# A fused linear-attention and squared-ReLU FFN kernel: the last token tile's FFN-out in two column halves, copied by two engines and stored from two queues

## The chip, the cores and the metric

The kernel runs on one core of one Trainium2 chip. A core has five engines, each with its own in-order instruction queue: TensorE (PE: matmuls, and PEld: the loading of a matmul's stationary operand), VectorE (DVE), ScalarE (ACT), GpSimd (POOL) and SyncE (SP), which only issues DMAs and handles semaphores. Matmul results land in PSUM, which has eight banks of 128 rows x 512 f32; the other engines copy from there to SBUF, and DMAs move data between SBUF and HBM. The metric is device time in microseconds (us).

## The reference

There are 8 batches, 8 heads, a sequence of 576 and a head dimension of 64. A learned feature map turns q and k into 256 features, linear attention follows, and its output (4608 tokens of 512) goes through an FFN with a squared ReLU.

```python
def phi(x):
    proj = np.einsum('bhsd,df->bhsf', x, w_phi)               # d = 64, f = 128
    proj = proj - np.max(np.abs(proj), axis=-1, keepdims=True)
    return np.concatenate([np.exp(proj), np.exp(-proj)], axis=-1)
q_p, k_p = (phi(q), phi(k))
kv = np.einsum('bhsf,bhsd->bhfd', k_p, v)
z = np.sum(k_p, axis=2)
num = np.einsum('bhsf,bhfd->bhsd', q_p, kv)
den = np.einsum('bhsf,bhf->bhs', q_p, z)[..., None] + 1e-06
x = (num / den)              # -> [4608, 512]
h = np.maximum(x @ w_in, 0.0)        # w_in [512, 2048]
return (h * h @ w_out).astype(np.float32)   # w_out [2048, 512]
```

## The kernel before

Attention is worked batch by batch (eight batches). Its feature matmuls contract over the 64 of the head dimension, so they use 64 rows of TensorE (lines 496, 588, 634 and 666); the numerator matmuls (L734), the transposes (L438, L765) and the whole FFN use 128 rows. The FFN works on token tiles of 128, in nine chunks of four tiles. FFN-in (L796) makes, for a chunk, 16 PSUM banks of 128 hidden units x 512 tokens, four matmuls each; ScalarE applies the ReLU (L801), and GpSimd, in the last chunks VectorE, squares it (L804, L807). FFN-out (L825) makes, for one token tile, one bank of 128 tokens x 512 outputs from 16 matmuls. These are given to the planner as four parts of four matmuls. VectorE copies the bank to an `ot` buffer (L832, a ring of two), and SyncE stores it as two DMAs of 64 rows (L837), since the two halves of a tile belong to different places in the output.

The order of instructions on each engine is written by a small planner, the class `Plan` (line 46). Every piece of work is an `op` with an engine, a planned cost, a latency until others may use its result, a sorting key, dependencies and the buffers that it takes. `order` plays the plan forward: each free engine takes the ready op with the lowest key for which buffers are free. The instructions are then written out in the order of their planned starts, and the waits between engines follow from which data and buffers they share, in that order. Planned times thus set only the order; the chip's own times come out of the waits.

For TensorE, `pick` (line 80) chooses between ops of 64 and of 128 rows, since a change between the two costs time. With `now` as the lowest key of the ready 128-row ops, it changes to 64 rows when the first of them is overdue (`LATE`), or when the first lies under `now + EARLY[0]` and the ready ones up to `now + EARLY[1]` sum to `GROUP`, 400 ns of work; it stays there as long as keys lie under `now + AHEAD`. While TensorE has nothing to do before the first FFN input is there, `fill` (line 51) puts warm-up matmuls (L392) into the plan, every 240 ns from 500 to 5500 planned ns.

Latencies depend on `slack`: 40 ns and 200 ns in the first two attention batches (`M0`), and `MARGIN` for the later ones and for the FFN. TensorE's latency is 350 ns where slack is 100 or more.

At the start GpSimd issues the loads of batch 0's k, v and q in pieces, then the weights (`FIRSTS`, line 368), and builds an identity matrix. SyncE loads w_phi (L342), VectorE fills constants (L329 to L332) and converts w_phi (L344), and ScalarE loads its function table (L337).

Of the kernel before, what the change touches and what calls it, by code (L numbers as in the profile page):

```python
# [45 lines left out]
class Plan:  # L46
# [2 lines left out]
        self.idle = {}  # L49

    def fill(self, eng, cost, period, fn, until):
        self.idle[eng] = [cost, period, fn, until, 0.0]

    def op(self, eng, cost, key, fn, deps=(), bufs=(), lat=0, rows=None):

# [19 lines left out]
    SWITCH = 96  # L75

    AHEAD, GROUP, LATE = 24, 400, 8
    EARLY = 3, 8

    def pick(self, q, rows, can):  # L80
        now = min((it[0] for it in q if it[2].rows == 128), default=None)
# [5 lines left out]
        else:  # L87
            go = half[0][0] < now - self.LATE
            if not go and half[0][0] < now + self.EARLY[0]:
                free, work = {}, 0  # L90
                for it in half:
                    if it[0] > now + self.EARLY[1]:
                        break
# [106 lines left out]
def kernel(  # L200
# [10 lines left out]
    nc = tc.nc  # L211

    B, H, S, D = q.shape
    Fd = w_phi.shape[1]
    DM, DF = moe_w_in.shape
    P = 128
    NPR = H // 2
    NJ = S // 64
    U = NPR * NJ
    M = U // 2  # L220
    KC1, KC2 = DM // P, DF // P
# [8 lines left out]
    def ring(name, n, shape, dtype, pool=sb):  # L230
        return Ring([pool.tile(shape, dtype, name=f"{name}{i}") for i in range(n)])

    wphi2 = sb.tile([P, Fd], BF16, name="wphi2")
    win = sb.tile([P, KC1, DF], BF16, name="win")
    wout = sb.tile([P, KC2, DM], BF16, name="wout")
    ident = sb.tile([P, P], BF16, name="ident")
    wphi_f = sb.tile([P, Fd], F32, name="wphi_f")
# [10 lines left out]
    r_ksh = ring("ksh", 2, [P, 2, 4, Fd], F32)  # L248
# [12 lines left out]
    r_ot = ring("ot", 2, [P, DM], F32)  # L261
# [10 lines left out]
    r_out = Ring([0, 1])  # L272

    pl = Plan()
    MARGIN = 200
    M0 = 40, 200, 350
    slack = [M0[0]]
    att = []
# [1 line left out]
    def pe(key, cost, fn, deps=(), bufs=(), rows=128):  # L280
        o = pl.op("pe", cost, key, fn, deps, bufs, lat=350 if slack[0] >= 100 else 240, rows=rows)
        att.append(o)
        return o

    def act(key, n, fn, deps=(), bufs=()):
        return pl.op("act", 60 + 0.83 * n, key, fn, deps, bufs, lat=220 - 70 * (slack[0] < 100) + slack[0])

    def dve(key, n, fn, deps=(), bufs=()):

        return pl.op("dve", 65 + 1.04 * n, key, fn, deps, bufs, lat=190 - 60 * (slack[0] < 100) + slack[0])  # L290
# [13 lines left out]
    def load(key, kb, rows, fn, deps=(), bufs=()):  # L304

        n = (queue[-1][0] if queue else 0) + rows
        full = [d for m, d in queue if m >= n - 4096][:1]
        i = pl.op("pool", 780, key, fn, list(deps) + (full if n > 4096 else []), bufs, lat=0)  # L310
        issues.append(i)
        d = pl.op("dma", kb * 3, key, None, [i], bufs, lat=2600)
        queue.append((n, d))
        return d
# [5 lines left out]
    def store(key, fn, deps=(), bufs=()):  # L320
        return pl.op("sp", 1200, key, fn, deps, bufs, lat=2400)

    pl.op("pool", 1250, -1e9, None)


    FIRST = -1000

    def begin():
# [5 lines left out]
                    "x (h m p) -> x h m p", h=2, p=64)[:, :, M], 0.0)  # L334

    o_begin = dve(FIRST - 2, 400, begin)
    act(FIRST - 2, 1400, lambda: nc.scalar.activation(  # L337
        out=scrap[:, 4:8], in_=scrap[:, 0:4], func=ACT.Exp), [o_begin])

    def ld_wphi():  # L340
        for e in range(2):
            nc.sync.dma_start(out=wphi_f[e * 64 : e * 64 + 64, :], in_=w_phi)  # L342

    o_wphi = dve(FIRST - 1, 130, lambda: nc.vector.tensor_copy(out=wphi2, in_=wphi_f),  # L344
                 [store(FIRST, ld_wphi)])

    src = {"k": (k, r_xk), "v": (v, r_xv), "q": (q, r_xq)}
    got = {}

    def load_x(b, name, key, dep=None, a=0, z=NPR):  # L350

        t, r = src[name]
        if (b, name) not in got:
            got[b, name] = Buf(r), []
        buf, parts = got[b, name]
        rows = t[b].rearrange("h s d -> (h s d)").rearrange("(pr t c) -> t pr c", pr=NPR, t=P)

        def fn():
            nc.gpsimd.dma_start(  # L359
                out=buf.t[:, a * NJ : z * NJ].rearrange("t (pr j) d -> t pr (j d)", j=NJ),  # L360
                in_=rows[:, a:z, :],
            )
        parts.append((a * NJ, load(key, 295 * (z - a), 128 * (z - a), fn, [dep], [buf])))

    win_v = moe_w_in.rearrange("(kc p) m -> p kc m", p=P)
# [5 lines left out]
    for n, what in enumerate(FIRSTS.split()):  # L371
        what, a = what.split(":")
        a, z = (int(x) for x in a.split("-"))
        at = FIRST + n if n < NEXT else -160 + n
        if what == "win":
            x = slice(a * P, z * P)
            o = load(at, 262 * (z - a), 512, lambda x=x: nc.gpsimd.dma_start(
                out=win[:, :, x], in_=win_v[:, :, x]))
            o_win.update({mc: o for mc in range(a, z)})
        elif what == "wout":  # L380
            o = load(at, 262 * (z - a), 128 * (z - a),
                     lambda a=a, z=z: nc.gpsimd.dma_start(out=wout[:, a:z], in_=wout_v[:, a:z]))
            o_wout.update({mc: o for mc in range(a, z)})
        else:
            load_x(int(what[1]), what[0], at, None, a, z)

    def loads(b, dep):
        for name in "kvq":
            load_x(b, name, 32 * b - 120, dep)
# [10 lines left out]
    chunks = [4] * 9  # L400
    first = [sum(chunks[:c]) for c in range(len(chunks))]
# [4 lines left out]
    jord = [pairs + [NJ - 1], [NJ - 1] + pairs]  # L406
# [8 lines left out]
    def attention(b, key):  # L415
# [43 lines left out]

        slack[0] = M0[b] if b < 2 else MARGIN  # L460
        tk = transposes(xk, lk, kT, 0)
# [7 lines left out]

        slack[0] = M0[b] if b < 2 else MARGIN  # L470
        nf = FG[b] if b < len(FG) else 0
# [311 lines left out]
    h2 = {}  # L783
# [29 lines left out]
    outv = out.rearrange("(b p j) n -> b j p n", p=64, j=NJ)  # L813
    op_buf, stores = {}, []

    def ffn_out(c, i, key):
        tt, part = i // 4, i % 4
        if part == 0:
            op_buf[0] = Buf(r_one), Buf(r_out)
        w, out_ = op_buf[0]  # L820
        mcs = range(part * 4, part * 4 + 4)

        def fn():
            for mc in mcs:
                nc.tensor.matmul(  # L825
                    out=w.t, lhsT=h2[c, mc, tt][0].t[:, h2[c, mc, tt][1] :][:, :P], rhs=wout[:, mc, :],
                    start=(mc == 0), stop=(mc == KC2 - 1))
        p_ = pe(key, 865, fn, [h2[c, mc, tt][2] for mc in mcs] + [o_wout[mc] for mc in mcs],
                [w, out_] + [h2[c, mc, tt][0] for mc in mcs])
        if part == 3:  # L830
            o = Buf(r_ot)
            d = dve(key - 2, 560, lambda: nc.vector.tensor_copy(out=o.t, in_=w.t), [p_], [w, out_, o])  # L832

            def fn():
                for u in range(2):
                    g = 2 * (first[c] + tt) + u
                    nc.sync.dma_start(out=outv[g // NJ, jord[g // NJ % 2][g % NJ]],  # L837
                                      in_=o.t[u * 64 : u * 64 + 64, :])
            stores.append(store(key, fn, [d], [o]))
# [4 lines left out]
    n = 0  # L844
# [40 lines left out]
    att.clear()  # L885
    slack[0] = MARGIN
    for n, (what, c, i) in units:
        (ffn_out if what else ffn_in)(c, *i, n)

    for o in paced:  # L890
        n = int(o.key) - LEAD
# [37 lines left out]
```

## Time and profile before

| what | value |
|---|---|
| four runs, median (lowest to highest) | 359.88 us (359.48 to 360.7) |
| the profiled execution, its own time | 359.71 us |
| its span in the profile | 357.9 us |
| TensorE busy | 347.6 us, 97% |
| VectorE, ScalarE, GpSimd busy | 246.2, 240.5, 187.0 us |
| granted TensorE clock | 1.0 |
| end of the last matmul | 353.28 us |
| end of the last VectorE copy | 354.00 us |

Times in the profile are microseconds from the start of the span. A group's row gives line, engine and operation, what is written and read with shape (partitions x elements) and type, the count, the busy time and the mean of one. Matmuls are pipelined: the mean of one (0.38 us for 512 columns) is the time from start to end, while the next starts 0.216 us after it. A timeline row gives start, duration, the instruction, and in brackets the idle time of the engine before it and what ended it. The chain of waits follows the work that ended last back to the start, and names the piece of work that each stretch of time went to.

### The profile page before, as it was taken

What the parts mean: (1) busy time and instruction counts of PE and PEld (TensorE: products, weight loads), DVE (VectorE), ACT (ScalarE), POOL (GpSimd) and SP (SyncE); (2) the same over time, 40 slices, a digit from 0 to 9 for tenths busy, and PEclk for the clock granted to TensorE, in tenths of its full rate; (3) what the DMA queues carried; (4) which work ended last, traced back from release to release, by engine and by line L of the source; (5) the groups of instructions that cost most, each with busy time, mean ns of one, the idle gap of its engine ahead of it and who ended that gap; (6) DMA issues with size and microseconds to landing.
All of it is one profiled execution on the core that took longest, in us unless ns stands there. A gap on an engine that the chain in (4) does not pass through costs nothing.

```text
span 357.9 us, 10261 instructions
## 1 busy us (share of the span) xinstructions
PE 347.6 (97%) x4051; PEld 198.3 (55%) x4051; DVE 246.2 (69%) x556; ACT 240.5 (67%) x485; POOL 187.0 (52%) x293
## 2 busy tenths in 40 slices
PE   8799899999999999999999999999999999999994
PEld 6669676676754555455545554555455544444441
DVE  2988978796889489867687789777977843333321
ACT  2898988589829972997569776896588833333300
POOL 8836964557827981689547754786536400000000
PEclk9999999999999999999999999999999999999999
DMA  7999982557945875479648756695441331121133
GB/s 101 203 210 208 208 154 60 90 83 129 204 91 107 143 138 105 94 125 205 105 88 146 160 114 88 115 196 104 83 97 33 68 69 29 29 59 31 29 76 71
DMA packets 68816, 39.79 MB, mean 111 GB/s; under 512 B 48672, under 2 KB 63136, under 8 KB 68768
## 3 DMA queue, kind: packets, MB, share of 16 engines
q0 software_dynamic: 15872, 18.35, 31.3%
q1 hardware_dynamic: 52896, 20.79, 29.5%
q8 instruction: 31, 0.51, 0.6%
q14 instruction: 17, 0.14, 0.1%
HBM read 36.77 MB, written 9.44 MB: 129 GB/s over the span
## 4 chain that ended last, share of the span: by engine, by line
PE 90%; DVE 4%; DMA 2%; ACT 2%; issue 1%; POOL 0%; POOLq 0%; DVEq 0%
PE one L796 35%; PE one L825 35%; PE one L734 6%; PE one L588 5%; PE one L496 3%; PE one L666 3%; PE one L634 3%; DMA xk<-in_k_dram 2%; DVE mk L507 1%; ACT qph L641 1%; PE one L438 1%; DVE m L673 1%; DVE qT L446 0%; DVE ksh L517 0%; POOL xk L359 0%
## 5 line engine op out<-in xcount | busy, mean ns | idle before, releaser
L804 POOL TENSOR_TENSOR h<-hr 128x512 bf16<-128x512 bf16 x112 | 115.3, 1041 | 81.2 <-ACT hr L801 75.6
L796 PE MATMUL one<-xT,win 128*128 128x512 bf16 (+2 forms) x768 | 145.1, 326 | 0.2 <-DVE m L687 0.2
L825 PE MATMUL one<-wout,h 128*128 128x512 bf16 x576 | 144.7, 379 | 0.4 <-DVE xo L755 0.3
L801 ACT ACTIVATE hr<-one 128x512 bf16<-128x512 f32 x144 | 85.0, 608 | 77.7 <-PE one L796 72.5
L796 PEld LDWEIGHTS <-win 128*128 128x128 bf16 x768 | 65.9, 98 | 49.3 <-issue 1.1
L825 PEld LDWEIGHTS <-h 128*128 128x128 bf16 x576 | 52.6, 98 | 58.5 <-issue 1.7
L641 ACT ACTIVATE qph<-one 128x512 bf16<-128x512 f32 (+1 forms) x160 | 77.0, 577 | 6.1 <-PE one L634 6.0
L525 ACT ACTIVATE kph<-ksh 128x1024 bf16<-128x1024 f32 (+1 forms) x68 | 61.2, 956 | 6.0 <-DVE ksh L517 5.8
L507 DVE TENSOR_REDUCE mk<-one 128x4 f32<-128x512 f32 (+1 forms) x80 | 49.6, 628 | 6.3 <-PE one L496 6.1
L687 DVE TENSOR_REDUCE m<-one 128x4 f32<-128x512 f32 (+1 forms) x60 | 35.3, 632 | 18.7 <-PE one L666 11.6
L517 DVE TENSOR_TENSOR ksh<-one,mk 128x512 f32<-128x512 f32 (+1 forms) x68 | 42.8, 629 | 3.6
L832 DVE COPY ot<-one 128x512 f32<-128x512 f32 x36 | 24.7, 687 | 29.3 <-PE one L825 29.3
L734 PEld LDWEIGHTS <-qph 128*128 128x128 bf16 x640 | 29.1, 97 | 15.9 <-issue 3.1
L734 PE MATMUL one<-kv_sb,qph 128*128 128x65 bf16 x640 | 33.6, 194 | 1.7 <-DVE one L744 1.4
L744 DVE TENSOR_TENSOR one<-one,em 128x260 f32<-128x260 f32 (+1 forms) x80 | 31.9, 429 | 4.3 <-PE one L734 3.8
L755 DVE TENSOR_TENSOR xo<-one,rden 128x256 bf16<-128x256 f32 (+1 forms) x80 | 31.6, 418 | 0.7
L807 DVE TENSOR_TENSOR h<-hr 128x512 bf16<-128x512 bf16 x32 | 13.6, 424 | 21.9 <-ACT hr L801 21.9
L696 POOL COPY mq<-m 64x4 f32<-64x4 f32 x108 | 20.2, 187 | 13.0 <-DVE m L687 9.6
L588 PE MATMUL one<-va,kph 64*128 64x65 bf16 x1152 | 23.6, 190 | 0.8 <-POOL va L555 0.8
L588 PEld LDWEIGHTS <-kph 64*128 64x128 bf16 x1152 | 21.1, 94 | 3.2 <-issue 3.0
L751 DVE RECIPROCAL rden<-one 128x4 f32<-128x4 f32 (+1 forms) x80 | 12.6, 175 | 14.2 <-PE one L734 13.8
L666 PE MATMUL one<-wphi,qT 64*128 64x128 bf16 x296 | 15.5, 217 | 0.3 <-DVE ksh L517 0.2
(45 smaller groups left out, 202.0 us busy)
## 6 DMA issues: line engine op xcount, KB each, us to landing
out_dram<-ot SPq DMA_DIRECT2D x72, 128.0 KB, 2.4
xk<-in_k_dram POOLq DMA_DIRECT2D x7, 576.0 KB, 6.6
xv<-in_v_dram POOLq DMA_DIRECT2D x7, 576.0 KB, 9.3
xq<-in_q_dram POOLq DMA_DIRECT2D x7, 576.0 KB, 12.2
win<-in_moe_w_in_dram POOLq DMA_DIRECT2D x2, 1024.0 KB, 15.7
wout<-in_moe_w_out_dram POOLq DMA_DIRECT2D x2, 1024.0 KB, 24.9
xv<-in_v_dram POOLq DMA_DIRECT2D x2, 288.0 KB, 7.3
xq<-in_q_dram POOLq DMA_DIRECT2D x2, 288.0 KB, 8.8
```

The lines of the kernel that those rows point to most:

```text
L507: nc.vector.tensor_reduce(out=mk.t[:, e, ms], in_=wv(e), axis=AX.X, op=ALU.max, apply_absolute_value=True)
L517: nc.vector.tensor_tensor(out=ksh.t[:, e, : n // 2, :], in0=wv(e), in1=mk.t[:, e, ms].to_broadcast([P, n // 2, Fd]), op=ALU.subtract)
L525: nc.scalar.activation(out=t.t[:, :, : n // 2, :].rearrange("x e i f -> x e (i f)"), in_=ksh.t[:, :, : n // 2, :].rearrange("x e i f -> x ...
L588: nc.tensor.matmul(out=kvp(w, hi)[:, 2 * prl + s], lhsT=kph[g][s].t[r, i % 2, i // 2, :], rhs=va[s if g < nf else 0].t[r, u, : D + 1], sta ...
L641: nc.scalar.activation(out=t.t.rearrange("f (r b) hi p -> f b r hi p", b=2)[:, bk, :, :, lo:hi_], in_=w[bk].t[:, : nj * 256].rearrange("f ...
L687: d1 = [dve(kk, nj * 256, lambda w=w, m0=m0, nj=nj, bk=bk: nc.vector.tensor_reduce(out=m0.t[:, bk, : 2 * nj], in_=w[bk].t[:, : nj * 256].r ...
L734: nc.tensor.matmul(out=w.t[:, z * P : z * P + D + 1], lhsT=qg[s].t[:, h // 2, h % 2, :], rhs=kv[r][0].t[:, z % 2, z // 2, s, :], start=(s ...
L744: nc.vector.tensor_tensor(out=x, in0=x, in1=em.t[lo:hi_, hs].to_broadcast(list(x.shape)), op=ALU.mult)
L796: nc.tensor.matmul(out=w.t[:, y * n : (y + 1) * n], lhsT=win[:, kc, mc * P : (mc + 1) * P], rhs=xT.t[:, a:z, kc, :], start=(kc == 0), stop ...
L801: o = act(key - 4, TCH, lambda: nc.scalar.activation(out=r.t, in_=w.t, func=ACT.Relu), [p_], [w, r])
L804: o = pool(key - 4, 1050, lambda: nc.gpsimd.tensor_tensor(out=t.t, in0=r.t, in1=r.t, op=ALU.mult), [o], [r, t])
L825: nc.tensor.matmul(out=w.t, lhsT=h2[c, mc, tt][0].t[:, h2[c, mc, tt][1] :][:, :P], rhs=wout[:, mc, :], start=(mc == 0), stop=(mc == KC2 - 1))
```

## The change

The last token tile's FFN-out keeps its four parts, but the first two parts now make columns 0 to 255 (eight of the 16 matmuls each, 256 columns wide) and the last two make columns 256 to 511, all in the same PSUM tile. After each half, VectorE copies rows 0 to 63 and ScalarE rows 64 to 127 of that half to an `ot` buffer; SyncE stores the former and ScalarE's own queue stores the latter. Other tiles are as they were.

With it come changes to the planner's numbers and to the start. Warm-up matmuls begin at 1100 planned ns. `EARLY` is (3.3, 7) for (3, 8), and `MARGIN` 220 for 200. The planner assumes that ScalarE and SyncE can't start before 740 ns and VectorE not before 500, as it did with 1250 for GpSimd. The op of the ScalarE table and the chain of w_phi are given to the planner after the loads, and the w_phi load has a planned latency of 1600 for 2400. `load_x` gets a branch that would load pieces over SyncE or ScalarE, for the pieces that `EARLY_X` lists; `EARLY_X` is empty.

```diff
     def fill(self, eng, cost, period, fn, until):
-        self.idle[eng] = [cost, period, fn, until, 0.0]
+        self.idle[eng] = [cost, period, fn, until, 1100.0]
...
-    EARLY = 3, 8
+    EARLY = 3.3, 7
...
-    MARGIN = 200
+    MARGIN = 220
...
-    pl.op("pool", 1250, -1e9, None)
+    for e, c in (("pool", 1250), ("act", 740), ("sp", 740), ("dve", 500)):
+        pl.op(e, c, -1e9, None)
...
-    act(FIRST - 2, 1400, lambda: nc.scalar.activation(
+    o_table = lambda: act(FIRST - 2, 1400, lambda: nc.scalar.activation(
...
-    o_wphi = dve(FIRST - 1, 130, lambda: nc.vector.tensor_copy(out=wphi2, in_=wphi_f),
-                 [store(FIRST, ld_wphi)])
+    o_wphi = lambda: dve(FIRST - 1, 130, lambda: nc.vector.tensor_copy(out=wphi2, in_=wphi_f),
+                         [pl.op("sp", 1200, FIRST, ld_wphi, lat=1600)])
...
+    EARLY_X = {}
...
+        if (b, name, a) in EARLY_X:
...
+            return
...
+    o_table()
+    o_wphi = o_wphi()
...
-        mcs = range(part * 4, part * 4 + 4)
+        end = c == len(chunks) - 1 and tt == chunks[c] - 1
+        mcs = range(part % 2 * 8, part % 2 * 8 + 8) if end else range(part * 4, part * 4 + 4)
+        cols = slice(part // 2 * 256, part // 2 * 256 + 256) if end else slice(0, DM)
 
         def fn():
             for mc in mcs:
                 nc.tensor.matmul(
-                    out=w.t, lhsT=h2[c, mc, tt][0].t[:, h2[c, mc, tt][1] :][:, :P], rhs=wout[:, mc, :],
-                    start=(mc == 0), stop=(mc == KC2 - 1))
+                    out=w.t[:, cols], lhsT=h2[c, mc, tt][0].t[:, h2[c, mc, tt][1] :][:, :P],
+                    rhs=wout[:, mc, cols], start=(mc == 0), stop=(mc == KC2 - 1))
...
-        if part == 3:
+        if end and part % 2:
+            o = Buf(r_ot)
+            for u, copy, eng in ((0, nc.vector.tensor_copy, nc.sync), (1, nc.scalar.copy, nc.scalar)):
+                rows = slice(u * 64, u * 64 + 64)
+                d = (act if u else dve)(key - 2, 256, lambda copy=copy, rows=rows: copy(
+                    out=o.t[rows, cols], in_=w.t[rows, cols]), [p_], [w, out_, o])
+                g = 2 * (first[c] + tt) + u
+
+                def fn(eng=eng, rows=rows, g=g):
+                    eng.dma_start(out=outv[g // NJ, jord[g // NJ % 2][g % NJ]][:, cols],
+                                  in_=o.t[rows, cols])
+                stores.append(pl.op("act" if u else "sp", 620, key, fn, [d], [o], lat=2400))
+        elif part == 3:
```

More of the change, by code (lines that the diff above doesn't have):

```diff
@@ L362, in fn @@
             )
+        if (b, name, a) in EARLY_X:
+            eng, n = EARLY_X[b, name, a]
+            stage = Buf(r_ksh)
+            flat_x = lambda: stage.t.rearrange("x e i f -> x (e i f)")[:, : (z - a) * NJ * D]
+            def fn():
+                (nc.scalar if eng == "act" else nc.sync).dma_start(
+                    out=flat_x().rearrange("t (pr c) -> t pr c", c=NJ * D), in_=rows[:, a:z, :])
+            i = pl.op(eng, 640, FIRST - 3 + n, fn, [], [stage, buf], lat=0)
+            d = pl.op("dma", 295 * (z - a) * 3, FIRST - 3 + n, None, [i], [stage, buf], lat=1400)
+            for e, (lo, hi) in enumerate(((0, 5), (5, NJ))):
+                def fn(e=e, lo=lo, hi=hi):
+                    (nc.scalar.copy if e else nc.vector.tensor_copy)(
+                        out=buf.t[:, a * NJ + lo : a * NJ + hi].rearrange("t j d -> t (j d)"),
+                        in_=flat_x()[:, lo * D : hi * D])
+                parts.append((a * NJ, (act if e else dve)(
+                    FIRST + 2 + n, (hi - lo) * D, fn, [d], [stage, buf])))
+            return
         parts.append((a * NJ, load(key, 295 * (z - a), 128 * (z - a), fn, [dep], [buf])))
```

## The prediction

> **What bounds the kernel now.** I read the page first, then busy time by stretches, then the chain of waits, and last the end and the start instruction by instruction.
>
> The page, its first lines and the slices of TensorE:
>
> ```profile
> span 357.9 us, 10261 instructions
> PE 347.6 (97%) x4051; PEld 198.3 (55%) x4051; DVE 246.2 (69%) x556; ACT 240.5 (67%) x485; POOL 187.0 (52%) x293
> ...
> PE   8799899999999999999999999999999999999994
> ```
>
> TensorE is the bound everywhere but in the first tenth and in the last slice. Busy time by stretches (us and number of instructions for each engine) says it more sharply:
>
> ```profile
> 40.00:60.00 20.00, 18.64 (x337) 13.12 (x337) 16.22 (x38) 18.32 (x44) 13.17 (x14) 1.00 0.74 129
> ...
> 140.00:180.00 40.00, 40.00 (x468) 21.03 (x464) 29.08 (x67) 29.91 (x59) 27.54 (x44) 1.00 0.75 127
> 180.00:220.00 40.00, 40.00 (x474) 21.04 (x469) 33.34 (x71) 30.18 (x57) 24.92 (x41) 1.00 0.66 121
> ...
> 338.60:353.30 14.70, 14.67 (x68) 6.46 (x66) 3.10 (x5) 0.60 (x1) 0.00 (x0) 1.00 0.33 72
> 353.30:357.90 4.60, 0.00 (x0) 0.00 (x0) 0.69 (x1) 0.00 (x0) 0.00 (x0) 1.00 0.26 57
> ```
>
> From 60 us to 353.3 us TensorE has no idle time to give back; the last 4.6 us hold one VectorE copy and stores. So a change can win in three places only: the last 4.6 us, the start, and, in between, in how TensorE's own work is put together. What that means is seen in the chain of waits (start, duration, what) of an ordinary stretch:
>
> ```profile
> 183.80 0.55 PE one L496 x16
> 184.35 0.97 PE one L796 x4
> 185.32 0.86 PE one L825 x4
> 186.18 0.86 PE one L796 x4
> ```
>
> Four FFN matmuls of 512 columns take 0.86 us (0.216 each); the four that follow a stretch of 64-row attention matmuls (L496, L588, L634, L666) take 0.97. A change of row height thus costs 0.11. Matmul by matmul I count 17, 18, 17 and 20 such changes in the four 40 us from 100 to 260 us, and 98 from 60 to 280 us.
>
> The end, chain and then timeline (SPq is SyncE's DMA issuing):
>
> ```profile
> 339.89 13.39 PE one L825 x62
> 353.28 0.03 issue
> 353.31 0.69 DVE ot L832
> ```
>
> ```profile
> 349.85 0.69 DVE L832 COPY ot<-one 128x512 f32<-128x512 f32 x1 [2.76 <-PE one L825]
> 350.57 4.56 SPq L837 DMA_DIRECT2D out_dram<-ot  x4
> 353.31 0.69 DVE L832 COPY ot<-one 128x512 f32<-128x512 f32 x1 [2.76 <-PE one L825]
> ```
>
> **The last tile before.** Let S be the start of its first matmul. 16 matmuls at 0.216: the last starts at S+3.24 and ends 0.38 later (mean of one, 379 ns), S+3.62. Copy: 0.03 to start, 0.69 long: S+4.34. SyncE issues the two 64-row stores one behind the other, 354.02 and 354.54: the second at S+4.89. From issue to landing the trace gives 2.25 and 2.36 for the two: S+7.25. From that landing to the end of the span 1.04: S+8.29, so S is at 349.65.
>
> **Part 1, the last tile after.** 32 matmuls of 256 columns in place of 16 of 512, in order: first half 16, second half 16. Their price is that of FFN-in's 256-column form: eight in 0.87 (0.109 each, own weight load hidden), one alone 273 ns. Without waits the 32 would take as long as the 16. But both halves lie in one PSUM tile. The planner sets the copies of the first half 350 ns (its latency for TensorE) after part 1 ends, while part 2 (planned at 865 ns) starts at once; so the written order is part 0, 1, 2, then the two copies, then part 3. If engines that touch the same PSUM bank are kept apart, the copies wait for part 2 and part 3 waits for the copies. The trace has nothing where TensorE writes one half of a bank while the other half is read, so I bound it: no wait at one end, the whole round trip at the other. The nearest rows are the numerator matmuls L734, which stood 0.80 until VectorE's L744 on their bank was done and started 0.04 after it, and L825, which stood 0.30 for VectorE's L755. They are other uses of the same kind of tile, but all wait; I take the wait.
>
> With it: 24 matmuls, the last starts at S+23 x 0.109 = S+2.51, ends S+2.78. Copies of 64 rows x 256 columns start at S+2.81. VectorE: 64x256 from PSUM took 0.419 in L755, 128x256 0.417 in L687, so 0.42, to S+3.23. ScalarE: 128x256 took 0.390 in L641, to S+3.20. I take the two to run side by side, since they read different rows; the other end is one behind the other. TensorE restarts at S+3.27: part 3's last matmul starts at +0.76, ends S+4.31. Behind the waiting matmul are only these eight. Copies to S+4.76 (VectorE) and S+4.73. Stores 0.03 later, now one each on SyncE and ScalarE, S+4.79; landing at 2.25 S+7.04; closing 1.04, S+8.08. **That is 0.21 less than S+8.29.** The parts: copy -0.27, second issue and its slower landing -0.63, TensorE's stall +0.65 (3.27 where the next start was due at 2.62), the matmuls' last end and rounding +0.04.
>
> Here a rule of the Trainium skill speaks against the change: "PSUM — Partial Sum Buffer", section on bank collisions, says that two engines must not touch one bank within the same 32 partitions at once, whatever the columns, and that different 32-partition groups may. By it the stall is certain and the two copies by rows may overlap, so the sum would be -0.21; by the other end of my bounds it would be -0.75.
>
> No wait at all: last matmul ends S+3.65. The second half takes the `ot` buffer of the tile before, whose stores landed at 352.83 and 353.45 (S+3.80), so the ScalarE copy can't start before S+3.83, ends S+4.22, is stored at S+4.25 and lands S+6.50: S+7.54, or -0.75. With the wait this buffer is free in time and costs nothing. One copy behind the other (ScalarE waits for VectorE, 0.43 more, twice): part 3 ends at S+4.74, last copy at S+5.62, landing 7.90 to 8.01, S+8.94 to 9.05: +0.7.
>
> The DMAs: SyncE issued 2 stores for the tile and issues 2 still; two go past it to ScalarE's queue. SyncE's first-half store goes at S+3.26, is issued in 0.59 at most, and its queue is free at S+4.79. ScalarE has no other work after 340 us (0.60 in the whole stretch above), so its copies and issues have cover. No DMA issued by ScalarE is in the trace: bounds are SyncE's own, 2.0 at least and 3.5 at most (the two small w_phi loads), so -0.2 to +1.1 around the stores' 2.25; I take the stores', the same rows to the same place.
>
> **Part 2, the start.** The warm-up matmuls of TensorE begin in the plan at 1100 ns, not 0. Planned arrival of the first piece of k is 1250+780+885+2600 = 5515; before, one at 0, one at 500 and then every 240 make 22, and the trace has 22. After it: 1100+240n < 5515, 19.
>
> ```profile
> 1.20 4.87 PE L392 MATMUL one<-ones 128*128 128x256 bf16 x22 [1.20 <-DVE scrap L330]
> ...
> 5.86 0.63 PE L438 MATMUL one<-ident,xk 128*128 128x128 bf16 x4
> ...
> 9.30 0.34 PE L438 MATMUL one<-ident,xk 128*128 128x128 bf16 x3 [0.55 <-DMA xk<-in_k_dram]
> ```
>
> At this point one takes 0.213, so three fewer free 0.64; the first k had landed at 4.69. But TensorE then stands idle for the third k load (landed 9.25, the piece of 6.18 us in the chain), and all later work follows from 9.30. The cover of the 0.64 is that load, whose issue on POOL is not moved. So 0; bounds -0.64 (all carried through) and +0.3 (a warm-up matmul or two put in front of an attention one). Moving the ScalarE table load and the w_phi conversion in the list, and the three start costs (740, 740, 500), changes planned times only: each is the first ready work of its engine either way. `EARLY_X` is empty, so its branch, with its loads and copies, issues nothing: 0.
>
> **Part 3, the order of the middle.** `MARGIN` 220 for 200 puts 20 ns on every planned ACT, DVE and POOL latency of FFN and of batches 2 to 7. TensorE's waits on others from 60 to 338 us sum to 0.2, so there is nothing for it to win; it hides under FFN matmuls at hand. `EARLY` 3.3, 7 for 3, 8 changes when TensorE may leave the FFN for a 64-row stretch: sooner (3.3 units ahead), but counting less work as ready (up to 7). One pulls to shorter stretches, the other to longer. The price is 0.11 a change, their number unknown. Bounds: all 40 us like the best (17) or the worst (20) or three beyond, +-3 changes x 5.5 x 0.11 = +-1.8. I take 0, in the middle, as the two limits pull apart. In the second batch (30 to 62 us) TensorE's waits for VectorE sum to 1.7; a new order may move those by some tenths either way.
>
> **Sum.** -0.21 + 0 + 0: span 357.7 for 357.94. The profiled execution took 359.71, 1.8 outside the span and 0.17 under the median 359.88. Forecast of the median: 359.7. What a measurement of this kernel tells from no change is about 0.3%, 1.08 us.
>
> **The rivals.**
> - *More changes of row height.* `EARLY`'s first number opens 64-row stretches before enough attention work is at hand, and they come out shorter. For it: 20 changes in 220 to 260 us where neighbours have 17. Against: the wait for 400 ns of ready work stays. Decides from 12 more changes (+1.3 - 0.2); at 2.5 per 40 us, 14 more: +1.5 - 0.2, **361.2**. This is the case on the slower side.
> - *Fewer changes*, through the second number: 12 fewer, -1.3 - 0.2, **358.4**.
> - *The start is carried through.* For it: k landed 1.2 before its transposes. Against: the idle time for the third load. -0.64 - 0.21, **359.0**.
> - *The copies go one behind the other*: +0.7, **360.6**. For it: both read one bank; against: different rows.
> - *The halves overlap*: the wait is my own reading and the change does all that two halves suggest; TensorE runs on while the first half is copied, -0.75, **359.1**. For it: the halves share no column. Against: every wait of L734 and L825 on a bank in use.
>
> **How the numbers follow.** Forecast 0.33, more changes 0.22, fewer 0.17, copies in turn 0.12, start 0.09, no wait 0.07. Faster by over 0.3%: nearly all of fewer (0.16), half of start (0.05, with a little help of the order), 0.03 from the rest: 0.24. Slower: more changes 0.20, part of copies in turn (0.06, with some more changes), 0.01: 0.27. Within: 0.49. Forecast and the two cases of the tail hold 359.1 to 360.6; eight in ten need both order cases: 358.2 (fewer changes, some of the start) to 361.5 (more changes, some of the copies in turn).
>
> **What would show it.** After: an idle time of TensorE of 0.6 to 0.7 in the last 4 us, ended by VectorE or ScalarE, and none of it if the no-wait case holds. VectorE copies of 0.42 and ScalarE copies of 0.39, starting together. Last landing 2.2 to 2.4 after both issues. Nineteen matmuls in the first warm-up row, and still an idle TensorE ended by the k load at about 9.3. The end of TensorE's work against 353.28: +0.7 from the stall, and all beyond it is the start and the changes of row height, which can be counted. The prediction is wrong if that count moves by more than ten, or if a store issued by ScalarE takes well over 2.4 to land.

## The result

| | before | after |
|---|---|---|
| timed runs, median (lowest to highest) | 359.70 us (358.67 to 360.97) | 360.67 us (359.56 to 362.55) |
| ratio to before, 95% interval | | 1.0028 (1.0019 to 1.0037) |
| span of the profiled execution | 357.94 us | 358.36 us |
| start of the first `ot` copy of FFN-out | 57.86 us | 57.30 us |
| start of the last tile's first matmul | 349.65 us | 349.92 us |
| from there to the end of the span | 8.29 us | 8.44 us |

The changed kernel is slower by 0.28%, about 1.0 us (0.7 to 1.3), where the prediction had it 0.2 us faster. That is small, but the interval leaves out 1: the loss is real. The last line of the table shows that the part the change is named for gives nothing; the two lines above it show that more is lost between 57 and 350 us (292.61 in place of 291.79), after a gain at the start.

The page of the kernel after, its first lines, TensorE's slices and the row of FFN-out:

```profile
span 358.4 us, 10307 instructions
PE 347.6 (97%) x4064; PEld 199.8 (56%) x4064; DVE 247.6 (69%) x557; ACT 243.5 (68%) x487; POOL 186.4 (52%) x293
...
PE   8799899999999999999999999999999999999994
...
L851 PE MATMUL one<-wout,h 128*128 128x512 bf16 (+1 forms) x592 | 144.6, 374 | 1.3 <-DVE ot L860 0.9
```

At this height nothing has moved, but for the new idle time at the end of the last row: 0.9 us in which FFN-out waits for the `ot` copies. (Line numbers move with the edits: FFN-out is L825 before and L851 here.) The end of the same kernel in the timeline (start, duration, instruction, in brackets the idle time before it and what ended it):

```profile
352.74 0.37 ACT L860 COPY ot<-one 64x256 f32<-64x256 f32 x1 [13.25 <-PE one L851]
353.13 0.55 ACTq L865 DMA_DIRECT2D out_dram<-ot  x1
353.14 0.42 DVE L860 COPY ot<-one 64x256 f32<-64x256 f32 x1 [2.33 <-ACT ot L860]
353.58 2.41 SPq L865 DMA_DIRECT2D out_dram<-ot  x2
353.61 1.03 PE L851 MATMUL one<-wout,h 128*128 128x256 bf16 x8 [0.91 <-DVE ot L860]
...
354.68 0.37 ACT L860 COPY ot<-one 64x256 f32<-64x256 f32 x1 [1.57 <-PE one L851]
355.07 0.48 ACTq L865 DMA_DIRECT2D out_dram<-ot  x1
355.08 0.42 DVE L860 COPY ot<-one 64x256 f32<-64x256 f32 x1 [1.52 <-ACT ot L860]
```

ScalarE copies its rows, and only then VectorE, whose wait is ended by `ACT ot`. TensorE's last eight matmuls start after both: 353.607, where the matmul before them had started at 352.429 and the next was due 0.109 later, so they are 1.07 late. The second pair of copies goes in turn again.

The start:

```profile
1.20 4.24 PE L416 MATMUL one<-ones 128*128 128x256 bf16 x19 [1.20 <-DVE scrap L331]
5.23 0.63 PE L462 MATMUL one<-ident,xk 128*128 128x128 bf16 x4
...
8.44 0.34 PE L462 MATMUL one<-ident,xk 128*128 128x128 bf16 x3 [0.34 <-DMA xk<-in_k_dram]
```

There are 19 warm-up matmuls and the first transposes come at 5.23, as worked out, but the third k load also landed at 8.39 where it had landed at 9.26.

An ordinary stretch in the chain of waits reads as before, 0.86 for four matmuls and 0.97 after a change of row height:

```profile
183.91 0.55 PE one L520 x16
184.47 0.97 PE one L820 x4
185.44 0.86 PE one L851 x4
```

The price of a change is thus the same; what differs is how many there are and where TensorE waits. In TensorE's written order I count 152 changes of row height before and 156 after (warm-up matmuls left out).

### The profile page after: what moved, and what is told of

Read it like the earlier page. It is cut to its first block, busy times and chain, and to the rows that moved or that the text cites. A ratio compares the mean times of both kernels' runs of the same rounds, so it can differ in the third digit from the quotient of the medians.

```text
span 358.4 us, 10307 instructions
## 1 busy us (share of the span) xinstructions
PE 347.6 (97%) x4064; PEld 199.8 (56%) x4064; DVE 247.6 (69%) x557; ACT 243.5 (68%) x487; POOL 186.4 (52%) x293
## 4 chain that ended last, share of the span: by engine, by line
PE 87%; DVE 6%; ACT 2%; DMA 1%; issue 1%; POOL 0%; DVEq 0%; POOLq 0%
PE one L851 35%; PE one L820 34%; PE one L758 6%; PE one L612 4%; PE one L520 3%; PE one L690 2%; PE one L658 2%; DVE mk L531 2%; DMA xk<-in_k_dram 1%; ACT qph L665 1%; DVE ksh L541 1%; DVE xo L779 1%; PE one L462 1%; DVE m L697 1%; DVE one L768 1%
## 5 line engine op out<-in xcount | busy, mean ns | idle before, releaser
L851 PE MATMUL one<-wout,h 128*128 128x512 bf16 (+1 forms) x592 | 144.6, 374 | 1.3 <-DVE ot L860 0.9
L825 ACT ACTIVATE hr<-one 128x512 bf16<-128x512 f32 x144 | 85.0, 605 | 72.7 <-PE one L820 64.7
L851 PEld LDWEIGHTS <-h 128*128 128x128 bf16 x592 | 53.8, 98 | 57.7 <-issue 3.5
L711 DVE TENSOR_REDUCE m<-one 128x4 f32<-128x512 f32 (+1 forms) x60 | 35.5, 630 | 21.0 <-PE one L690 14.6
L758 PEld LDWEIGHTS <-qph 128*128 128x128 bf16 x640 | 30.5, 97 | 18.2 <-issue 3.2
L758 PE MATMUL one<-kv_sb,qph 128*128 128x65 bf16 x640 | 35.3, 194 | 1.7 <-DVE one L768 1.4
L697 DVE TENSOR_REDUCE m<-one 128x4 f32<-128x512 f32 (+1 forms) x20 | 13.1, 682 | 3.6 <-PE one L690 3.4
```

The costliest lines, as they stand in the source:

```text
L711: d1 = [dve(kk, nj * 256, lambda w=w, m0=m0, nj=nj, bk=bk: nc.vector.tensor_reduce(out=m0.t[:, bk, : 2 * nj], in_=w[bk].t[:, : nj * 256].r ...
L758: nc.tensor.matmul(out=w.t[:, z * P : z * P + D + 1], lhsT=qg[s].t[:, h // 2, h % 2, :], rhs=kv[r][0].t[:, z % 2, z // 2, s, :], start=(s ...
L825: o = act(key - 4, TCH, lambda: nc.scalar.activation(out=r.t, in_=w.t, func=ACT.Relu), [p_], [w, r])
L851: nc.tensor.matmul(out=w.t[:, cols], lhsT=h2[c, mc, tt][0].t[:, h2[c, mc, tt][1] :][:, :P], rhs=wout[:, mc, cols], start=(mc == 0), stop=( ...
```

## The experiments

**One part at a time.** Four kernels: the tail alone; `MARGIN` alone; the start alone; and all but the tail.

```diff
 # tail_only: the kernel before with the diff of ffn_out
 # margin_only
-    MARGIN = 200
+    MARGIN = 220
 # start_only: the kernel after with MARGIN = 200, EARLY = 3, 8 and the old ffn_out
 # all_but_tail: the kernel after with the old ffn_out
```

> The kernel before with the new last tile alone; all else as before. Theory 1 (the copies go in turn, ScalarE then VectorE, and TensorE waits for both, so the tail gives nothing): from the first matmul of the last tile to the end 8.4 us where before has 8.3, so the time +0.1 to +0.2 us, ratio 1.000 to 1.001; TensorE starts its last eight matmuls 1.07 late. Rival (the tail carries the whole loss of about 1.0 us in the timed runs): ratio 1.003.

Measured: 0.9993 (0.9979 to 1.0008). The end is as in the change: ScalarE's and VectorE's copies at 353.70 and 354.10, the last eight matmuls 1.07 late, 8.43 from the last tile's start to the end. So the tail alone neither carries the loss nor gives a gain.

> The kernel before with MARGIN 220 for 200 alone. In the written order of TensorE this makes 156 changes between 64-row and 128-row matmuls where before has 152, all four of them after the second batch. Theory 1 (the order of the middle carries the loss): +0.7 to +0.8 us, ratio 1.002; the first matmul of the last tile starts at 350.4 where before has 349.65, give or take the start of the run. Rival (the tail or the start carries it): ratio 1.000.

Measured: 1.0034 (1.0020 to 1.0048), about +1.2 us (0.7 to 1.7): `MARGIN` alone carries the whole loss. The rows of all 36 `ot` copies, first the kernel before, then this one (count, shortest, median and longest in ns, start of the first and of the last):

```profile
L832 DVE COPY ot<-one x36: 673/691/693, 57.9 to 353.3; 128x512 f32<-128x512 f32 x36
```

```profile
L832 DVE COPY ot<-one x36: 660/691/693, 57.6 to 353.9; 128x512 f32<-128x512 f32 x36
```

The same 36 tiles take 295.45 us before and 296.26 with `MARGIN` 220 (from the copies' starts), +0.81; in the changed kernel the first 35 take 292.82 where before has 291.99, the same +0.83. `EARLY` has no part in this: with `EARLY` 3.3, 7 alone the written orders of all five engines are those of before, instruction by instruction, and in the profiles margin_only and all_but_tail, which differ in `EARLY`, run the same sequence on every engine.

Where the 0.81 lies can be counted over the trace. A change of row height costs the distance to the next matmul beyond what it is without the change: 0.10 into 64 rows, 0.12 to 0.20 out of them. From the first `ot` copy to the last tile they sum, at the median price of each kind, to 13.5 us in the profiles of the old order and to 14.25 in the three of the new one, +0.75: two more pairs, and four more of the dearest kind, out of a 256-column L634. TensorE's waits of over 70 ns outside the 64-row stretches sum to 0.59 before and 0.81 with 220, +0.22. Three places make that up: a new wait at 113.5, 0.39 more than before has there; 0.14 in a change of row height at 206.4; and, the other way, 0.32 less at 132.8, where before waits and 220 does not. The timeline of the new wait with `MARGIN` 220:

```profile
112.81 1.08 ACT L801 ACTIVATE hr<-one 128x512 bf16<-128x512 f32 x2
...
113.46 1.02 PE L796 MATMUL one<-xT,win 128*128 128x512 bf16 x4 [0.33 <-ACT hr L801]
```

FFN-in's matmuls wait until ScalarE's ReLU has read the bank that they are to write. All three profiles with this order (margin_only, all_but_tail, after) have it, 0.49 long; before has 0.10 at the same place, with the matmuls running on:

```profile
110.63 3.72 PE L796 MATMUL one<-xT,win 128*128 128x512 bf16 x16
```

Changes and waits together give +0.97. Within the 64-row stretches, counted likewise, the matmuls take 0.15 less than before, which leaves the 0.82 measured. (From the first `ot` copy to the last tile both orders run the same number of matmuls of each kind, so nothing else is left over.)

> The kernel before with the changes at the start alone: warm-up from 1100 planned ns, the start costs of ScalarE, SyncE and VectorE, table and w_phi ops given later. 19 warm-up matmuls ahead of the first transposes where before has 22; the same changes of row height as before. Theory 1 (the third k load bounds the start, and its early landing at 8.4 in the profile after was chance): 0, ratio 0.999 to 1.001, with the load landing anywhere between 8.3 and 9.3. Rival (fewer warm-up matmuls bring the start 0.6 forward in every run): -0.6 us, ratio 0.998.

Measured: 0.9988 (0.9974 to 1.0003), on the side of a gain but not clear of nothing. The profiles say more about the time up to the first `ot` copy. Two things vary there from run to run: when the third load lands, and when the granted clock becomes full. Where the clock was full at 6.3 to 7.0 us and the load landed at 8.28 to 8.51, the kernels with 22 warm-up matmuls (margin_only, own_ot, one_copy, two_queues) start the first `ot` copy at 57.60 to 57.64; before, with its load at 9.26, has 57.86. With the new start and 19, start_only has 57.24 (clock at 7.0, load 8.58), best 57.51 (clock at 6.8, load 8.87) and after 57.30 (clock at 5.9, load 8.39). Where the clock was full earlier, both come sooner: 57.34 and 57.38 with 22 (margin_230 at 3.9, margin_260 at 5.3), 56.45 with 19 (all_but_tail at 4.4). So the new start gives 0.1 to 0.4 up to there where the load is early, which it mostly is (by 8.9 in ten of the fourteen profiles). That a late load takes the gain away is not shown: no profile with 19 has it later than 8.87.

Nor does start_only's profile keep its gain. In one of its 64-row stretches TensorE pauses, which costs 0.50 and is in no other profile with this order:

```profile
197.47 0.23 PE L612 MATMUL one<-va,kph 64*128 64x65 bf16 x4 [0.34 <-issue]
```

The profile names nothing that TensorE waited for ("issue"). Its last tile starts at 349.53, where own_ot, one_copy and two_queues, with the old start, have 349.39 to 349.42. A single profile can thus hold a pause of this size that its order doesn't explain. Both theories were half right.

> The changed kernel with the old last tile: the start, EARLY and MARGIN stay. Theory 1: the order's +0.7 to +0.8 less or plus what the start does, so ratio 1.002 if the start does nothing, 1.0005 if the start gives its 0.6 in every run. Rival (the tail carries the loss): ratio 1.000 or below.

Measured: 1.0029 (1.0013 to 1.0045), the changed kernel's own ratio without its tail, and nearer to the end of the forecast where the start does nothing. Its profile gains 1.41 up to the first `ot` copy and then takes 1.51 more for the 36 tiles: the 0.82 of this order, and one further wait of 0.70 before FFN-out's matmuls at 162.25, which the other two profiles with this order don't have.

**Why the copies go in turn and TensorE waits.** Two kernels: a buffer of its own for each copy, and a bank of its own for the second half.

```diff
 # own_ot: the new tail, but
+    r_oe = ring("oe", 4, [P, DM], F32)
-            o = Buf(r_ot)
             for u, copy, eng in (...):
+                o = Buf(r_oe)
 # two_banks: the new tail, and
+        if end and part == 2:
+            op_buf[0] = Buf(r_one), Buf(r_out)
+            w, out_ = op_buf[0]
```

> The kernel before with the new last tile, where each of the four copies has an ot buffer of its own (four further buffers, used by the last tile alone). Theory 1 (the two copies of a half go in turn because they read one PSUM bank): as before, VectorE's copy starts only when ScalarE's has ended, about 0.40 after it, and TensorE's last eight matmuls come 1.07 late. Rival (they go in turn because they write one ot buffer): the two start within 0.1 of each other and TensorE's delay falls to about 0.68.

```profile
352.24 0.37 ACT L837 COPY oe<-one 64x256 f32<-64x256 f32 x1 [13.25 <-PE one L828]
...
352.64 0.42 DVE L837 COPY oe<-one 64x256 f32<-64x256 f32 x1 [2.33 <-ACT oe L837]
...
353.11 1.03 PE L828 MATMUL one<-wout,h 128*128 128x256 bf16 x8 [0.90 <-DVE oe L837]
```

VectorE still starts 0.40 after ScalarE, still released by ScalarE's copy, and TensorE is still 1.07 late. So it isn't the `ot` buffer; what the two copies still share is the PSUM tile that they read, at different rows. A tile here fills one bank, so "bank" and "tile" can't be told apart in these runs. This kernel ran only once, for its profile, so it has no ratio.

> The kernel before with the new last tile, the second half in a PSUM bank of its own; copies by rows on two engines and stores as in the change. Theory 1 (one bank makes TensorE wait): TensorE has no wait in the last tile and ends 3.65 after its start; ScalarE's second copy waits until the stores of the tile before have left its ot buffer (3.80), then the copies go in turn, and from the last tile's start to the end it is 7.5 us where before has 8.29: -0.8 us, ratio 0.998. Rival (TensorE waits for the copies for another reason, such as the h or ot buffers): still 1.07 late, 8.4 us, ratio 1.000.

TensorE's 32 matmuls now run without a wait, and from the last tile's start to its last matmul's end it is 3.66: the shared bank was what held it. The timeline of the second pair of copies:

```profile
354.94 0.37 ACT L839 COPY ot<-one 64x256 f32<-64x256 f32 x1 [1.85 <-DMA out_dram<-ot]
355.33 0.48 ACTq L844 DMA_DIRECT2D out_dram<-ot  x1
355.33 0.42 DVE L839 COPY ot<-one 64x256 f32<-64x256 f32 x1 [1.80 <-ACT ot L839]
```

They go in turn still, and the first waits for the store that has to leave its `ot` buffer, until 4.16 after the tile's start, later than the 3.80 expected. To the end it is 7.83, a gain of 0.46 on before where 0.8 was expected; ratio 0.9986 (0.9970 to 1.0002), of the same size but not clear of nothing.

**Copies by columns on one engine.** VectorE copies all 128 rows of a half; once with the bank shared, once with all causes removed.

```diff
 # one_copy: the new tail, but
+            d = dve(key - 2, 256, lambda: nc.vector.tensor_copy(
+                out=o.t[:, cols], in_=w.t[:, cols]), [p_], [w, out_, o])
+            for u, eng in ((0, nc.sync), (1, nc.scalar)):   # the two stores
 # best: that, with two banks, buffers from r_oe, the new start, and
     MARGIN = 200
```

> The kernel before with the two halves in one bank as in the change, but each half copied by VectorE alone over all 128 rows; the two stores as in the change. Theory 1 (a copy's time goes by columns, not rows, so the split by rows only puts a second copy behind the first): copy of 0.42, TensorE's delay falls from 1.07 to 0.66, and from the last tile's start to the end 7.7 us where before has 8.29: -0.6 us, ratio 0.998 to 0.999. Rival (a copy of 128 rows takes twice one of 64): copy of 0.8, 8.4 us, ratio 1.000.

```profile
352.22 0.42 DVE L834 COPY ot<-one 128x256 f32<-128x256 f32 x1 [1.93 <-PE one L827]
...
352.70 1.03 PE L827 MATMUL one<-wout,h 128*128 128x256 bf16 x8 [0.52 <-DVE ot L834]
```

128 rows take 0.425, 64 rows 0.416, while 512 columns took 0.691: a VectorE copy's time goes by its columns. TensorE is 0.68 late in place of 1.07. To the end 7.99 us, 0.31 better than before; 0.6 was expected, since of two stores issued at one moment ScalarE's took 2.18 to land. Ratio 0.9997 (0.9982 to 1.0012): in the timed runs no difference.

> Of the change: the start, EARLY, but MARGIN 200; the last tile in halves with a bank each and ot buffers of its own, each half copied by VectorE alone and stored from two queues. Theory 1: from the last tile's start to the end 7.1 us where before has 8.29, so -1.2 us, and the start's -0.4 as measured: ratio 0.995 to 0.997. Rival (the DMAs set the end whatever the copies do): 7.7 or more, ratio 0.998 or above.

Measured: 0.9955 (0.9938 to 0.9972), 1.6 us faster than before. TensorE has no wait, the last copy takes 0.42 from 353.01, and it is 7.33 from the last tile's start to the end: 0.96 less than before, of the 1.2 expected. It is the one kernel of these that is clearly faster than before.

**The second queue by itself.**

```diff
 # two_queues: the kernel before, for the last tile's second store
-                    nc.sync.dma_start(
+                    nc.scalar.dma_start(
```

> The kernel before, where the second of the last tile's two stores is issued by ScalarE and all else is as before: one copy, no halves. Theory 1 (of the tail only the second queue was a gain, about 0.5 to 0.6): from the start of the copy of the tile before to the end 7.5 us where before has 8.09, ratio 0.998 to 0.999. Rival (the stores share the same DMA engines and land no earlier): 8.0 to 8.1, ratio 1.000.

```profile
L838 SPq DMA_DIRECT2D out_dram<-ot x1: 466/466/466, 353.8 to 353.8; - x1
L838 ACTq DMA_DIRECT2D out_dram<-ot x1: 551/551/551, 353.8 to 353.8; - x1
...
DMA to landing us min/median/max: 2.3/2.5/2.6
```

Both stores are issued together, 0.5 sooner for the second, but it lands 2.62 after its issue where SyncE's took 2.36. From the start of the copy of the tile before to the end it is 7.89 in place of 8.09: of the 0.5, 0.2 is left. Ratio 1.0001 (0.9985 to 1.0018).

**Is it the number of changes?** Three more values of `MARGIN` in the kernel before, chosen by the changes in the written order.

```diff
-    MARGIN = 200
+    MARGIN = 160   # and 260, 230
```

> The kernel before with MARGIN 160 alone. TensorE's written order has 176 changes of row height where before has 152. Theory 1 (the loss from MARGIN goes by the number of changes, 0.12 to 0.14 us each after the second batch): +3.0 to +3.4 us, ratio 1.008 to 1.0095. Rival (it goes by the latency assumed: 220 lost because it is more cautious, and 160 is bolder): no loss or a gain, ratio 1.000 or below; a second rival (shorter planned latencies make TensorE wait): far more than 3.4, seen as waits of TensorE rather than as changes.

Measured: 1.0133 (1.0104 to 1.0162), about +4.8 us, from three runs. The fourth, the profiled one, took 371.58 with a granted clock of 0.95 almost throughout, so its length is not compared. Its trace has 134 changes from the first `ot` copy on, where before has 111, and 0.16 of waits in all. So the bolder plan loses, and the rival by latency falls. But the loss is above the 1.008 to 1.0095 of the theory: about 1.4 us are left over (0.3 at the least), and since the only profile ran at the lower clock, nothing shows what they are.

> The kernel before with MARGIN 260 alone: 168 changes of row height where before has 152. Theory 1 (by the number of changes): +2.0 to +2.3 us, ratio 1.0055 to 1.0065. Rival (by the latency assumed, in proportion to 220's loss): +2.5 to +3.0, ratio 1.007 to 1.008.

Measured: 1.0041 (1.0027 to 1.0054), less than the theory and the rival had.

```profile
L832 DVE COPY ot<-one x36: 656/691/692, 57.4 to 354.5; 128x512 f32<-128x512 f32 x36
```

297.1 us for the 36 tiles, 1.6 more than before. Counted over the trace: changes +2.2, waits -0.5 (0.09 for 0.59). The changes alone would have been 0.6 too dear.

> The kernel before with MARGIN 230 alone: 150 changes of row height where before has 152 and MARGIN 220 has 156. Theory 1 (by the number of changes): -0.1 to -0.3 us, ratio 0.999 to 1.000. Rival (by the latency assumed): worse than 220, ratio 1.004 or above.

Measured: 1.0039 (1.0017 to 1.0061): the theory of changes alone falls. The number is the rival's, but the rival had 160 without a loss and 260 at 1.007 or more, and both were measured otherwise. The order has two changes less, and in the trace they cost 0.1 less; the 36 tiles take 0.8 more all the same. The timeline of its one profile shows where:

```profile
111.11 0.59 ACT L801 ACTIVATE hr<-one 128x512 bf16<-128x512 f32 x1
...
111.75 1.02 PE L796 MATMUL one<-xT,win 128*128 128x512 bf16 x4 [0.73 <-ACT hr L801]
```

It is the same kind of wait as with 220, FFN-in for a bank that the ReLU still reads, 0.80 over the usual spacing; waits over 70 ns sum to 1.03, +0.44, and one more in a 64-row stretch at 131.1 adds 0.4. Together that is +0.76, and +0.77 was measured. So the theory is mended: a written order costs its changes of row height and its waits for banks, and `MARGIN` moves both, without a rule for which way. With 220 both went up, changes by the larger part; three profiles agree on that. For 230 the waits rest on one profile, and after the pause in start_only it isn't shown that both belong to the order.

## Why the prediction was wrong

- **Part 3, the order of the middle, is the step that failed.** It said of `MARGIN`: "it hides under FFN matmuls at hand", and took 0. Alone it costs 0.81 us in the profile, and the timed runs have 1.0034: four more changes of row height (+0.75) and more waits for banks (+0.22), less 0.15 within the 64-row stretches. "Nothing for it to win" was right; that a new order could lose was asked of `EARLY` only, not of `MARGIN`. The rival of more changes came in, by the wrong parameter: `EARLY` changes nothing at all. Its limit of 12 more changes was too high: four were enough for +0.75, because of their kinds and since a price of 0.11 was too low for those out of 256 columns (0.20). Its count of 98 from 60 to 280 us was an error too; the trace has 109.
- **Part 1, TensorE's wait, was right in kind** (two_banks has none), and so was the written order of parts and copies. "I take the two to run side by side" was wrong: they go in turn, 0.40 apart, twice. The rival's matmul end, S+4.74, was measured at S+4.72. Its sum, +0.7, was too high, since the smaller stores landed 1.92 to 1.95 after issue, not 2.25 to 2.36, and the closing took 0.92 for 1.04: +0.15 in all. The stated reason for side by side was that the rows differ; the section of the Trainium skill's "PSUM — Partial Sum Buffer" on bank collisions, drawn on there, would allow it between groups of 32 partitions. No run here shows the chip's side of this: the waits written into this program keep apart the engines that touch one PSUM tile, which is one bank, and that decided. The stall of TensorE, a term of +0.65, came out at +1.07, and the tail at +0.15 in place of -0.21; the larger part of the miss is `MARGIN`'s.
- **Part 2, the start**: 19 warm-up matmuls and transposes at 5.23 were right. "So 0" left out a gain of 0.1 to 0.4 up to the first `ot` copy, which the timed runs of the start alone don't tell from nothing; the load that was to hide it landed at 9.26 in the one profile at hand, and by 8.9 in ten of the other thirteen.
- **The sum.** Forecast -0.21 + 0 + 0. Measured parts: tail +0.15, start -0.1 to -0.4, middle +0.82, together +0.6 to +0.9; the timed runs have +1.0 (0.7 to 1.3). The profiled execution has +0.41, since it was 0.56 ahead at the first copy, with its load early. Whether the timed runs have something beyond the parts isn't settled. The further wait of 0.70 in all_but_tail could be part of it; that was not tried.
- **Issues on ScalarE**: taken as SyncE's stores, they landed after 1.94 to 2.62, within the bounds given.

## What to carry to other kernels

Where an order is written by a planner, a small change of a planning constant is a new program: compare its switches and its buffer waits with the old one before looking at what the change was named for. In a program whose waits are set as in this one, a PSUM tile that is read in halves while the other half is written needs a bank for each half, and a VectorE copy should be split by columns, not rows, as its time goes by columns. One profile's DMA landing is one draw, and a step that is hidden by it is hidden only in that draw.

## What the runs showed of the hardware that was not expected

In two profiles of fourteen (tail_only and two_banks) the granted clock fell to half for 3.41 us just after TensorE's idle time in the second batch. Busy time by stretches of tail_only, the column before the last two is the clock:

```profile
38.00:42.00 4.00, 2.52 (x48) 2.18 (x45) 3.52 (x10) 4.00 (x13) 4.00 (x5) 1.00 1.24 209
42.50:45.90 3.40, 3.40 (x24) 1.31 (x24) 2.27 (x5) 3.05 (x7) 3.40 (x5) 0.51 1.21 207
46.00:50.00 4.00, 4.00 (x98) 3.48 (x92) 2.95 (x7) 3.12 (x6) 1.48 (x2) 1.00 1.21 208
```

In that stretch 512-column matmuls start 0.427 apart, not 0.216, and the first `ot` copy comes at 59.11, 1.2 to 1.8 later than in the profiles with 22 warm-up matmuls and a full clock after the start. The kernel before has the same idle time (2.61 busy of the same 4 us) without the fall in its profile. What makes the clock fall in the one and not in the other isn't shown. The fall costs as much as all that this change did, and it is why profiled spans are compared here by stretches and not whole.
